# Scores of sparse attention made one step earlier, and three early weight splits put into other steps

## The chip, the cores and the metric

The kernel runs on one core of a Trainium2 chip. The metric is the device time of one launch in microseconds (us), as the median of several runs; lower is better. One further execution was profiled, and the rows shown below are its trace. The engines are named PE (matrix multiplications, with PEld for its weight loads), DVE (vector engine), ACT (scalar engine), POOL (GpSimd) and SP (which issues most DMAs).

## The reference

Block-sparse attention and, on its output, a mixture of experts. Cut to what matters:

```python
B, H, S, D = 4, 8, 768, 64                 # 24 blocks of 32 rows
scores = q @ k.T / sqrt(D)
mask: key blocks 0 and 23, the own block and its neighbours, three random blocks per query block;
      query blocks 0 and 23 see every key
attn = exp(scores - max); attn /= attn.sum + 1e-9; x = attn @ v
x -> (3072 tokens, 512); logits = x @ w_gate (8 experts); e = argmax(logits)
gate = softmax(logits)[e]; eom = sigmoid(x @ w_output_gate)[e]
out = gate * eom * (relu(x @ w1[e]) @ w2[e])         # 512 -> 1024 -> 512
```

## The kernel before

**Two stages.** Attention runs first, to about 300 us. Each expert's tokens are then gathered into slots of 128 rows, and 28 slots go through the two layers of their expert, to the end. Weights and tokens are held there as a high and a low half in fp16. `w_h` (ACT, L924) makes the high half of a piece of weights, `w_l` (DVE, L930) the low one. Nine pieces are split during attention already, in two halves of 512 columns each, in steps that the table `AHEAD` (L53) lists: for each piece the steps of `w_h`, `w_l`, `w_h`, `w_l`.

**Steps.** Attention is done in two halves (`bp` 0 and 1), each for two of the four batches. A half has 8 dense units (the two query blocks that see everything) and 11 tiles (`i`) of two query blocks. A tile has four sparse units, two pairs; the units of a pair, the even and the odd one, differ in the batch (`b`), the pairs in the group of heads (`hg`). So there are 104 units, and unit m has its step m. A unit's operations are spread over steps by lags:

- step m: `pS`, the scores S on PE (L490); the first unit of a pair makes those of both, 32 matmuls. `dM`, the maximum (DVE, L497). `aE`, the exp (ACT, L502), which leaves P
- step m+2: `pT`, four transposes of P (PE, L441) into T; the copy of T to pt, on ACT for the even unit (`aH`, L448), on DVE for the odd one (`dL`, L450)
- step m+3: `pO`, the product with the values (PE, L515 for the common and window blocks, vc; L522 for the random ones, vt)
- step m+4: `aO`, the copy of O (ACT, L531), and `dD`, the sums of a row (DVE, L427); m+5: `fin`, their reciprocal (DVE, L540); m+6: `fin2`, the scaling into x (POOL)

Within a step the loop at L1181 to L1203 emits these in one fixed order: `pT`, `pS`, `aH`, the early hooks, `dM`, `dL`, `pO`, `aO`, `aE`, `dD`, `fin`, the other hooks, `fin2`. Every engine works its instructions off in the order in which they were emitted (`in_order`, L77); only semaphores let engines run apart.

**Hooks.** `at(step, f)` puts further work into a step: DMAs, gathers of keys and values, the splits of `AHEAD`, and the router. The keys of a tile lie in one of three rings `kr`: three random blocks each, copied by DVE (L381), ACT (L383) and POOL (L385), and the window's four, copied by DVE (`window_k`, L392 and L393). `lead` (L1062) says how many steps ahead. The random values vt are gathered by POOL's indirect DMA (`gather_v`, L403) into one of two buffers.

**The router's turn** of a finished tile of x: transposes xp (PE, L677), the cast to the high half (ACT, L679), the subtraction for the low half (DVE, L680), the logits lp (PE, L689 and L690), their sum lsum (DVE, L694). After every fourth tile follow the choice of experts on POOL and DVE and the sum of ranks rp (PE, L732 to L737).

**Banks.** Scores S share four PSUM banks with lp, rp and the transition's small tiles. T shares two banks with xp; the pool assigns them, not in strict turn. In a tile with a router's turn, xp stands in the last step of the tile before; the T of the first unit's step takes the bank that DVE's copy of the T before it (an odd unit's) frees, and the T of the next step takes that same bank once ACT has copied it. O has two banks of its own.

Of the kernel before, what the change touches and what calls it, by code (L numbers as in the profile page):

```python
# [49 lines left out]
PACE = -1, 0, 0, 2, 4, 7, 8, 9, 10, 11, 12, 13, 14, 15, 16, 17, 18  # L50

PLAN = 6, (20,)
AHEAD = ((73, 74, 77, 78), (81, 82, 85, 86), (89, 90, 93, 94), (96, 97, 97, 98), (97, 98, 98, 99), (99, 100, 100, 101),  # L53
         (100, 101, 101, 102), (101, 102, 102, 103), (103, 104, 104, 105))
FIN = ("_1_9_1_1", "_1_10_0_1", "_1_10_1_1")
T0 = 5
# [34 lines left out]
def tile_kernel(ctx, tc, q, k, v, sampled, wg, wcat, out):  # L91
# [911 lines left out]
    def at(n, f, *a):  # L1003
        hooks.setdefault(n, []).append((f, a))
# [45 lines left out]
    for bp in range(2):  # L1050
# [6 lines left out]
        for i in range(NPAIR):  # L1057
            u0 = o + 8 + 4 * i
            if bp or i != 1:
                at(u0 - 8, load_q, bp, i)  # L1060

            lead = 3 if bp or i > 1 else 0  # L1062
            for kind, n, ns in KC[bp]:
                at(u0 - n - lead if bp or i != 1 else u0 - min(n, 5), gather_k, bp, i, kind, ns)
            at(u0 - 3 - lead, window_k, bp, i)
            at(u0 - 5 + LAGS[2] if bp or i else 6, window_v, bp, i)
            at(u0 - 5 + LAGS[2] if bp or i > 1 else (8, 12)[i], gather_v, bp, i)
# [43 lines left out]
    for m, un in enumerate(units):  # L1111
        lags = LAGD if isinstance(un, Dense) else LAGS
        le, lt, lo = lags
        d = "0" if isinstance(un, Dense) else ""
        for lag, f in ((lt, "pT"), (0, "pS"), (lt, "aH"), (0, "dM"), (lt, "dL" + d), (lo, "pO"), (lo + 1, "aO"), (lo + 1, "dD"),
                       (le, "aE" + ("0" if le else "")), (lo + 2, "fin"), (lo + 3, "fin2")):
            sched.setdefault((min(m + lag, n + 2), f), []).append(getattr(un, f.strip("0")))

# [51 lines left out]

    for i, hl in enumerate(AHEAD):
        for m in range(2):
# [91 lines left out]
```

## Time and profile before

| | |
|---|---|
| median of 3 runs | 623.2 us (621.53 to 624.46) |
| profiled execution | 622.91 us, its span 621.0 us |
| mean granted PE clock | 0.970 |
| PE busy | 564.4 us (91%) |
| PEld busy | 391.3 us (63%) |
| DVE busy | 473.8 us (76%) |
| ACT busy | 435.5 us (70%) |
| POOL busy | 260.6 us (42%) |

A row of a timeline reads: start in us from the start of the span, duration, engine, line of the kernel, operation, what it writes and reads (sizes as partitions x elements, and how many instructions the row joins), and in square brackets how long the engine had stood idle and what ended that, by the profile. A releaser in brackets is the last semaphore that the profile saw, so it can name an instruction that had ended long before. A row of windows reads: the stretch, its length, then busy time and count of instructions of PE, PEld, DVE, ACT and POOL, the granted PE clock, a DMA share and GB/s. A row of waits reads: waiting operation, releaser, total time, how many, the longest.

### The profile page before, as it was taken

The page shows a single profiled execution, that of the slowest core. Times are in us where ns is not written, and L with a number is a line of the kernel's source. Part 1 is how long each engine was busy: PE and PEld are TensorE (multiplying, and loading weights), DVE is VectorE, ACT ScalarE, POOL GpSimd, SP SyncE. Part 2 cuts the span into 40 slices and gives each one's busy share as a digit, 9 for nine tenths or more (in the row PEclk, how much of TensorE's full clock was granted, in tenths as well). Part 3 has the DMA queues.
Part 4 walks back from the last instruction along what each step waited for, and adds up shares of the span by engine and source line. Part 5 has one row for each costly group of instructions (what it writes and reads, how often), then busy time and mean ns, then how long its engine had stood idle before and what let it go on. Part 6 is the DMA issues. An engine that isn't in the chain of part 4 may idle for free. (4 is left out here: it accounts for less than half of the span.)

```text
span 621.0 us, 22116 instructions
## 1 busy us (share of the span) xinstructions
PE 564.4 (91%) x8275; PEld 391.3 (63%) x8275; DVE 473.8 (76%) x934; ACT 435.5 (70%) x834; POOL 260.6 (42%) x324
## 2 busy tenths in 40 slices
PE   6799988989889888888979998999999999999996
PEld 4466655555556555555757776777777777777763
DVE  4587657567657567577689988899898989989891
ACT  1466657656557777677459887887888888788871
POOL 4575758765645766665332131131312122131311
PEclk8899989999889899998699999999999999999999
DMA  8986979795865866559227399359943935823491
GB/s 312 381 260 228 320 250 296 274 283 134 285 141 204 257 210 189 176 159 272 53 64 286 83 292 357 83 145 275 301 119 95 309 76 163 265 63 81 94 295 45
DMA packets 72859, 126.94 MB, mean 204 GB/s; under 512 B 38187, under 2 KB 44459, under 8 KB 72492
## 3 DMA queue, kind: packets, MB, share of 16 engines
q1 hardware_dynamic: 61004, 87.84, 47.9%
q0 software_dynamic: 11744, 37.64, 18.2%
q8 instruction: 67, 1.10, 0.7%
q14 instruction: 44, 0.36, 0.2%
HBM read 183.09 MB, written 20.49 MB: 328 GB/s over the span
## 5 line engine op out<-in xcount | busy, mean ns | idle before, releaser
L930 DVE SCALAR_TENSOR_TENSOR kr<-r,kr 128x1024 f16<-128x1024 f32 (+1 forms) x173 | 184.5, 1110 | 17.2 <-ACT kr L924 16.2
L924 ACT ACTIVATE kr<-r 128x1024 f16<-128x1024 f32 (+1 forms) x173 | 156.4, 960 | 0.8 <-DMA r<-in_wcat_dram 0.8
L941 PEld LDWEIGHTS <-kr 128*128 128x128 f16 x2004 | 125.9, 98 | 46.8 <-issue 9.2
L981 POOL DMA_INDIRECT out_dram<-yo,tab x28 | 29.7, 1059 | 213.2 <-ACT yo L978 191.1
L972 PE MATMUL y<-kr,hh 128*128 128x512 f16 x423 | 114.0, 379 | 0.4 <-DVE hh L959 0.4
L502 ACT ACTIVATE P<-S,mx 128x256 f32<-128x256 f32 x176 | 74.5, 478 | 46.1 <-DVE mx L497 42.4
L941 PE MATMUL h<-xb,kr 128*128 128x128 f16 x1344 | 93.3, 219 | 2.1 <-DMA xb<-qz 2.1
L497 DVE TENSOR_REDUCE mx<-S 128x2 f32<-128x512 f32 x88 | 59.9, 680 | 30.2 <-PE S L490 30.1
L930 DVE SCALAR_TENSOR_TENSOR ws<-r,ws 128x1024 f16<-128x1024 f32 (+1 forms) x60 | 67.8, 1167 | 8.7 <-ACT ws L924 7.1
L403 POOL DMA_INDIRECT vt<-vscr,vidx x44 | 46.8, 1063 | 55.7 <-PE O L522 45.0
L441 PE MATMUL T<-ident,P 128*128 128x128 f32 x352 | 58.7, 291 | 11.1 <-DVE den L540 6.6
L972 PEld LDWEIGHTS <-hh 128*128 128x128 f16 x594 | 50.0, 98 | 25.7 <-DVE hh L959 1.1
L490 PE MATMUL S<-kr,qz 64*32 64x256 f32 x1408 | 59.4, 400 | 4.3 <-issue 3.8
L924 ACT ACTIVATE ws<-r 128x1024 f16<-128x1024 f32 (+1 forms) x60 | 58.1, 1015 | 0.8 <-PE y L972 0.8
L941 PEld LDWEIGHTS <-ws 128*128 128x128 f16 x684 | 44.3, 100 | 16.9 <-issue 6.1
L952 ACT ACTIVATE hh<-h 128x512 f16<-128x512 f32 (+1 forms) x56 | 30.5, 545 | 33.6 <-PE h L941 31.0
L441 PEld LDWEIGHTS T<-ident,P 128*128 128x128 f32 x352 | 38.8, 145 | 18.0 <-issue 14.0
L522 PE MATMUL O<-vt,pt 128*32 128x65 f32 x1408 | 42.0, 229 | 8.6 <-issue 4.6
L515 PEld LDWEIGHTS O<-vc,pt 128*64 128x64 f32 x704 | 28.7, 140 | 31.2 <-issue 20.8
L680 DVE TENSOR_TENSOR xT<-xp,xT 128x512 f16<-128x512 f32 x24 | 16.6, 692 | 39.4 <-ACT xT L679 36.2
L972 PE MATMUL y<-ws,hh 128*128 128x512 f16 x171 | 46.0, 379 | 0.0
L515 PE MATMUL O<-vc,pt 128*64 128x65 f32 x704 | 41.1, 238 | 3.2 <-DVE den L427 1.3
(227 smaller groups left out, 931.1 us busy)
## 6 DMA issues: line engine op xcount, KB each, us to landing
r<-in_wcat_dram SPq DMA_DIRECT2D x240, 512.0 KB
vscr<-vn SPq DMA_DIRECT2D x12, 520.0 KB
qz<-in_q_dram SPq DMA_DIRECT2D x24, 256.0 KB
xscr<-xq SPq DMA_DIRECT2D x48, 128.0 KB
vc<-vscr SPq DMA_DIRECT2D x22, 260.0 KB
kn<-in_k_dram SPq DMA_DIRECT2D x2, 1536.0 KB
vs<-in_v_dram SPq DMA_DIRECT2D x6, 512.0 KB
kn<-in_k_dram SPq DMA_DIRECT2D x6, 512.0 KB
```

The lines of the kernel that those rows point to most:

```text
L403: nc.gpsimd.indirect_dma_start(t[:, s].rearrange("p b j w -> p (b j w)"), None, vscr[bp], bass.IndirectOffsetOnAxis(ap=vidx[:, i, s:s + 1] ...
L441: nc.tensor.transpose(pt[:, 128 * c:128 * c + 128], p[:, 128 * c:128 * c + 128], ident)
L490: nc.tensor.matmul(u.s[64 * h2 + 32 * qi:64 * h2 + 32 * qi + 32, hp], t[p, 64 * j + 32 * qi:64 * j + 32 * qi + 32], g[p, 1 - qi:3:1 + qi, ...
L497: nc.vector.tensor_reduce(mx, self.s, axis=AX.X, op=ALU.max, negate=True)
L502: nc.scalar.activation(p[:, 256 * hp:256 * hp + 256], self.s[:, hp], AF.Exp, bias=self.mx[:, hp:hp + 1])
L515: nc.tensor.matmul(o[64 * h2:64 * h2 + 64, hp, 0:VW], w[:, col:col + 64], cv[:, b, 4 * h2 + 2 * hg + hp], start=hp == 0, stop=False)
L522: nc.tensor.matmul(o[64 * h2 + 32 * qi:64 * h2 + 32 * qi + 32, hp, 0:VW], w[:, col:col + 32], av[:, qi, b, 4 * h2 + 2 * hg + hp], start=Fa ...
L924: nc.scalar.activation(w[:, 0, r], piece(n // 8, n % 8)[:, r], AF.Copy, scale=SW)
L930: nc.vector.scalar_tensor_tensor(w[:, 1, r], piece(n // 8, n % 8)[:, r], SW, w[:, 0, r], op0=ALU.mult, op1=ALU.subtract)
L941: nc.tensor.matmul(hps[n // 4][:, 128 * j:128 * j + 128], w[:, hl, 128 * c:128 * c + 128], x[:, c // 2, xl, c % 2], start=cnt == 0, stop=c ...
L952: nc.scalar.activation(hs[g][0], hps[g][:, 0:m], AF.Relu)
L972: nc.tensor.matmul(ys[s], a[:, m], w[:, l, 512:1024], start=n % 8 == 0 and cnt == 0, stop=n % 8 == 7 and cnt == 2)
```

## The change

Three edits. `pS` of the sparse units stands at lag -1 instead of 0: the scores of a pair are made in the step in front of the pair's first unit. `lead` becomes 4 instead of 3 (for tile 1 of the first half 1 instead of 0; tile 0 of the first half keeps 0), so the keys' copies move a step earlier with them. And in the first three entries of `AHEAD` each `w_l` stands two steps later; the `w_h` and the six other entries stay.

```diff
-AHEAD = ((73, 74, 77, 78), (81, 82, 85, 86), (89, 90, 93, 94), (96, 97, 97, 98), (97, 98, 98, 99), (99, 100, 100, 101),
+AHEAD = ((73, 76, 77, 80), (81, 84, 85, 88), (89, 92, 93, 96), (96, 97, 97, 98), (97, 98, 98, 99), (99, 100, 100, 101),
          (100, 101, 101, 102), (101, 102, 102, 103), (103, 104, 104, 105))
...
-            lead = 3 if bp or i > 1 else 0
+            lead = 4 if bp or i > 1 else 1 if i else 0
             for kind, n, ns in KC[bp]:
                 at(u0 - n - lead if bp or i != 1 else u0 - min(n, 5), gather_k, bp, i, kind, ns)
             at(u0 - 3 - lead, window_k, bp, i)
...
         le, lt, lo = lags
+
+        ls = 0 if isinstance(un, Dense) else -1
         d = "0" if isinstance(un, Dense) else ""
-        for lag, f in ((lt, "pT"), (0, "pS"), (lt, "aH"), (0, "dM"), (lt, "dL" + d), (lo, "pO"), (lo + 1, "aO"), (lo + 1, "dD"),
+        for lag, f in ((lt, "pT"), (ls, "pS"), (lt, "aH"), (0, "dM"), (lt, "dL" + d), (lo, "pO"), (lo + 1, "aO"), (lo + 1, "dD"),
```

What this does to the order of the engines shows in three places. The first is PE at tile 4 of the second half, four steps from the step of its first unit on. In the names, `S_1_4_0_1` is half 1, tile 4, batch 0, heads 1; the matmuls of one S alternate between the pair's two units, and of them the first row stands here. Before:

```order
L677 MATMUL xp14_5072<-ident_82,x1_1_4896 128x2x64 x4
L441 MATMUL T0_1_3_0_1_5079<-ident_82,P_1_3_0_1_4995 128x128 x4
L490 MATMUL S_1_4_0_0_5084<-kr1_180,qz2_186 32x256
...
L515 MATMUL O_1_3_1_0_5108<-vc1_183,pt0_1_3_1_0_5038 64x65 x4
...
L441 MATMUL T0_1_3_1_1_5154<-ident_82,P_1_3_1_1_5054 128x128 x4
...
L689 MATMUL lp14_5195<-wg32_91,xT14_5071 128x32
...
L441 MATMUL T0_1_4_0_0_5207<-ident_82,P_1_4_0_0_5123 128x128 x4
L490 MATMUL S_1_4_0_1_5212<-kr1_180,qz2_186 32x256
...
L441 MATMUL T0_1_4_1_0_5283<-ident_82,P_1_4_1_0_5178 128x128 x4
L515 MATMUL O_1_4_0_0_5292<-vc0_182,pt0_1_4_0_0_5230 64x65 x4
```

And with the change:

```order
L677 MATMUL xp14_5111<-ident_82,x1_1_4907 128x2x64 x4
L441 MATMUL T0_1_3_0_1_5118<-ident_82,P_1_3_0_1_5019 128x128 x4
L515 MATMUL O_1_3_1_0_5129<-vc1_183,pt0_1_3_1_0_5066 64x65 x4
...
L441 MATMUL T0_1_3_1_1_5165<-ident_82,P_1_3_1_1_5082 128x128 x4
L490 MATMUL S_1_4_0_1_5170<-kr1_180,qz2_186 32x256
...
L689 MATMUL lp14_5237<-wg32_91,xT14_5110 128x32
...
L441 MATMUL T0_1_4_0_0_5249<-ident_82,P_1_4_0_0_5144 128x128 x4
L515 MATMUL O_1_3_1_1_5258<-vc1_183,pt0_1_3_1_1_5190 64x65 x4
...
L441 MATMUL T0_1_4_1_0_5293<-ident_82,P_1_4_1_0_5207 128x128 x4
L490 MATMUL S_1_5_0_0_5298<-kr2_181,qz0_184 32x256
```

The scores of the tile's second pair (`S_1_4_0_1`) now stand ahead of the logits lp, one step earlier, and those of the next tile's first pair stand in this tile's last step. So between the T of steps 0 and 1 only an O is left, and the same between those of steps 2 and 3; an S stands between those of steps 1 and 2, and one between that of step 3 and the next tile's xp.

The second place is DVE in the same tile, from the maximum of its first unit to the copy of the last step. Before:

```order
L497 TENSOR_REDUCE mx_1_4_0_0_5106<-S_1_4_0_0_5084 128x2
...
L497 TENSOR_REDUCE mx_1_4_1_0_5159<-S_1_4_1_0_5085 128x2
L450 COPY pt0_1_3_1_1_5161<-T0_1_3_1_1_5154 128x512
...
L694 TENSOR_REDUCE lsum_187<-lp14_5195 128x16
L497 TENSOR_REDUCE mx_1_4_0_1_5232<-S_1_4_0_1_5212 128x2
...
L392 TENSOR_SCALAR kr0_179<-kn1_1061 128x256
L393 TENSOR_SCALAR kr0_179<-kn1_1061 128x768
L930 SCALAR_TENSOR_TENSOR ws0_4949<-r0_3611,ws0_4949 128x512
L497 TENSOR_REDUCE mx_1_4_1_1_5288<-S_1_4_1_1_5213 128x2
L450 COPY pt0_1_4_1_0_5290<-T0_1_4_1_0_5283 128x512
```

And with the change:

```order
L497 TENSOR_REDUCE mx_1_4_0_0_5127<-S_1_4_0_0_5046 128x2
...
L930 SCALAR_TENSOR_TENSOR ws0_4991<-r0_3635,ws0_4991 128x512
L497 TENSOR_REDUCE mx_1_4_1_0_5188<-S_1_4_1_0_5047 128x2
L450 COPY pt0_1_3_1_1_5190<-T0_1_3_1_1_5165 128x512
...
L392 TENSOR_SCALAR kr0_179<-kn1_1083 128x256
L393 TENSOR_SCALAR kr0_179<-kn1_1083 128x768
L694 TENSOR_REDUCE lsum_187<-lp14_5237 128x16
L497 TENSOR_REDUCE mx_1_4_0_1_5256<-S_1_4_0_1_5170 128x2
...
L497 TENSOR_REDUCE mx_1_4_1_1_5316<-S_1_4_1_1_5171 128x2
L450 COPY pt0_1_4_1_0_5318<-T0_1_4_1_0_5293 128x512
```

The window's copies (L392, L393) have gone from step 2 to step 1, and the weight split (L930) from step 2 to step 0. Nothing is added between the last two maxima.

The third place is PE behind a router sum, rp3 in tile 6 of the second half, with the semaphores that a row waits for in brackets. Before:

```order
L737 MATMUL rp3_5672<-cum4_192,ones_93 128x2
L441 MATMUL T0_1_5_1_1_5692<-ident_82,P_1_5_1_1_5575 128x128 [waits Activation_49]
L441 MATMUL T0_1_5_1_1_5692<-ident_82,P_1_5_1_1_5575 128x128 x3
L515 MATMUL O_1_5_0_1_5701<-vc1_183,pt0_1_5_0_1_5622 64x65 [waits DVE_49]
```

And with the change:

```order
L737 MATMUL rp3_5682<-cum4_192,ones_93 128x2
L441 MATMUL T0_1_5_1_1_5703<-ident_82,P_1_5_1_1_5603 128x128 [waits Activation_49]
L441 MATMUL T0_1_5_1_1_5703<-ident_82,P_1_5_1_1_5603 128x128 x3
L490 MATMUL S_1_6_0_1_5708<-kr0_179,qz1_185 32x256
L490 MATMUL S_1_6_1_1_5709<-kr0_179,qz1_185 32x256 [waits DVE_49,Activation_49]
```

The scores of the second pair now follow rp and T directly. Their second matmul waits for DVE and ACT, because rp has taken one bank of the four and it gets the bank of the tile's first unit, which that unit's exp has to have read.

## The prediction

> **What bounds the kernel now.** I read the windows by stage first, then the waits of each engine between 20 and 322 us, then the timelines of single tiles. A tile here is four sparse units in four steps, called step 0 to 3, counted from the step that takes the maximum of its first unit.
>
> ```profile
> 200.00:250.00 50.00, 42.43 (x919) 28.57 (x911) 33.35 (x101) 35.40 (x97) 34.31 (x43) 0.97 0.72 223
> 450.00:500.00 50.00, 50.00 (x553) 35.82 (x550) 45.89 (x47) 41.08 (x56) 9.90 (x8) 1.00 0.60 171
> ```
>
> From 322 us on PE has no idle time (second row, 50.00 of 50), and the change touches nothing there: what attention saves or loses moves that part as a whole. In attention (first row; the columns are PE, PEld, DVE, ACT, POOL) PE leads with 42.43 of 50 and idles 7.6. So the sum is made of PE's stops before 322 us.
>
> ```profile
> DVE mx L497 <- PE S L490: 30.1, 30, 2.5
> PE T L441 <- DVE den L540: 6.6, 10, 1.7
> PE T L441 <- issue: 2.3, 2, 1.4
> PE T L441 <- DVE mx L497: 1.3, 1, 1.3
> PE T L441 <- DVE den L427: 0.9, 1, 0.9
> ```
>
> The largest wait of DVE, 30.1 us for the scores S, is no loss by itself, since DVE isn't the bound. It counts where PE waits for DVE later: the transposes T stop PE for 6.6 + 2.3 + 1.3 + 0.9 = 11.1 us. One such tile, DVE and ACT first, then PE:
>
> ```profile
> 221.22 0.69 DVE L497 TENSOR_REDUCE mx<-S 128x2 f32<-128x512 f32 x1 [1.21 <-PE S L490]
> 221.95 0.84 ACT L502 ACTIVATE P<-S,mx 128x256 f32<-128x256 f32 x2 [0.32 <-DVE mx L497]
> 222.09 0.56 DVE L393 TENSOR_SCALAR kr<-kn 128x768 f32<-128x768 f32 x1
> 222.56 0.69 DVE L930 SCALAR_TENSOR_TENSOR ws<-r,ws 128x512 f16<-128x512 f32 x1
> 223.16 0.69 DVE L497 TENSOR_REDUCE mx<-S 128x2 f32<-128x512 f32 x1
> 223.76 0.69 DVE L450 COPY pt<-T 128x512 f32<-128x512 f32 x1
> 223.15 0.66 PE L677 MATMUL xp<-ident,x 128*128 128x128 f32 x4
> 224.59 0.63 PE L441 MATMUL T<-ident,P 128*128 128x128 f32 x4 [0.79 <-DVE den L540]
> ```
>
> In step 2 DVE stands 1.21 us without scores, then does the maximum, the window of keys (L392, L393), a weight split (L930), the next maximum and the copy of step 3's T, without a gap. The copy ends at 224.45; the T of the next step 0, which takes the copied bank, starts 0.14 later, 0.79 late. Three of these stops lie past 270 us, where weight splits that stay where they are fill DVE:
>
> ```profile
> 278.22 0.63 PE L441 MATMUL T<-ident,P 128*128 128x128 f32 x4 [1.71 <-DVE den L540]
> 291.19 0.63 PE L441 MATMUL T<-ident,P 128*128 128x128 f32 x4 [0.98 <-DVE den L540]
> 293.50 1.12 PE L441 MATMUL T<-ident,P 128*128 128x128 f32 x4 [0.94 <-issue]
> ```
>
> **The change part by part.** The sum is made against the profiled execution's own 622.9 us (span 621.0), which lies 0.3 under the median 623.2.
>
> **Scores one step earlier, window out of step 2, three splits to step 0: the T stops go.** DVE then comes to step 2 with its scores made and without window and split. What is left ahead of the copy is two maxima and small work, so the copy ends as soon as its own T allows, and between T and the next T stand S, O and xp of step 3. PE's pace, start to start:
>
> ```profile
> 192.33 0.45 PE L515 MATMUL O<-vc,pt 128*64 128x65 f32 x8
> 193.08 0.66 PE L677 MATMUL xp<-ident,x 128*128 128x128 f32 x4
> 194.17 0.63 PE L441 MATMUL T<-ident,P 128*128 128x128 f32 x4 [0.43 <-DVE den L540]
> 198.55 0.64 PE L441 MATMUL T<-ident,P 128*128 128x128 f32 x4
> 199.12 1.09 PE L490 MATMUL S<-kr,qz 64*32 64x256 f32 x32
> 200.14 0.45 PE L515 MATMUL O<-vc,pt 128*64 128x65 f32 x8
> ```
>
> T takes 0.57, S 1.02, O 0.75. T, S and O of step 3 are thus 2.34 us, against 1.3 for T and its copy one behind the other (0.63 + 0.69 = 1.32 by the rows at 224.59 and 223.76): no stop remains. Of 11.1 us the three late ones (1.71 + 0.98 + 0.94 = 3.63) stay, 7.5 go. Ends: 0, if something else makes DVE late, and 7.5.
>
> **Values gathered a little earlier for their use.** POOL issues the gathers of vt when the O of step 2 two tiles ahead of their use is done; the O of step 3 needs them five steps later.
>
> ```profile
> 94.92 0.95 POOL L403 DMA_INDIRECT vt<-vscr,vidx  x1 [0.30 <-issue]
> 95.77 0.63 PE L441 MATMUL T<-ident,P 128*128 128x128 f32 x4 [0.85 <-DVE den L427]
> 104.88 0.43 PE L522 MATMUL O<-vt,pt 128*32 128x65 f32 x14 [1.27 <-issue]
> 84.32 0.43 PE L522 MATMUL O<-vt,pt 128*32 128x65 f32 x14 [2.69 <-DMA vt<-vscr,vidx]
> 135.45 0.43 PE L522 MATMUL O<-vt,pt 128*32 128x65 f32 x14 [1.22 <-DMA vt<-vscr,vidx]
> 203.78 0.43 PE L522 MATMUL O<-vt,pt 128*32 128x65 f32 x14 [1.62 <-issue]
> ```
>
> About 10 us pass from issue (94.92) to the matmul that had waited (104.88): the landing ends these four stops, 6.8 us together. In the changed order one more S (1.02 us) lies on PE between issue and use, and the T stops that lay there are gone. At 84.32 that is worth 1.02; at 104.88 1.02 - 0.85 = 0.17; at 203.78 1.02 - 0.43 = 0.59; at 135.45, between these, I take 0.6. Sum 2.4. Ends: 0, if the landing itself comes later, and 6.8.
>
> **New wait: T of step 1 behind T of step 0.** No S stands between them any more, and the later one takes the bank that ACT's copy of the earlier one frees. That copy is queued behind the router's cast (L679), which waits for xp.
>
> ```profile
> 105.24 0.66 PE L677 MATMUL xp<-ident,x 128*128 128x128 f32 x4
> 105.73 0.60 PE L441 MATMUL T<-ident,P 128*128 128x128 f32 x4
> 105.93 0.59 ACT L679 CAST xT<-xp 128x512 f16<-128x512 f32 x1 [1.02 <-PE xp L677]
> 106.43 0.59 ACT L448 COPY pt<-T 128x512 f32<-128x512 f32 x1
> 106.55 0.69 DVE L680 TENSOR_TENSOR xT<-xp,xT 128x512 f16<-128x512 f32 x1 [1.07 <-issue]
> ```
>
> Here ACT stood ready: cast 0.69 after xp's start, copy end at 107.02, 1.78 after it, plus the 0.14 above: 1.92. PE comes after xp (0.49 to 0.58), T and O 1.81 to 1.90 after it. That is a stop of 0 to 0.1, taken as 0.1 in 20 tiles: +2.0. ACT would have to be late for more (a rival below); at 224 us it was, its cast 2.2 us after xp, but because its exp had waited for the late maximum, which the change takes away. Queued behind the waiting T on PE are S and O of step 1, and DVE's and ACT's next units wait for them.
>
> **New wait: S for a bank, in the four tiles that hold a router sum.** The router sum rp takes one of four score banks in step 0, and the second matmul of the S in step 1 then gets the bank of the tile's first unit, whose exp was done long before and now comes first.
>
> ```profile
> 187.63 0.18 PE L732 MATMUL rp<-oh,tri 128*128 128x8 f16 x1
> 187.99 0.64 PE L441 MATMUL T<-ident,P 128*128 128x128 f32 x4
> ```
>
> From xp's start: cast at 0.69, router subtraction 0.62 later (105.93 to 106.55), maximum 0.60 later (as 223.16 to 223.76), exp 0.73 later (221.22 to 221.95) and 0.84 long, PE 0.14 later: 3.62. PE gets there after xp 0.58, T 0.57, O 0.75, rp 0.36 and T 0.57: 2.83. Stop 0.8, four times: +3.2; ends 0 (DVE has its maximum earlier) and, with ACT late by as much again, 4 x 1.6.
>
> **The rest.** ACT's and POOL's gathers of keys and DVE's window keep their count and their distance to the scores; both move a step. SP's order is unchanged, and so is each DMA. At the first step of each half the scores now stand ahead of a dense O and wait for a dense exp: between 0 and one S (1.02) each, +0.5 for both. Past 270 us the third split enters step 0 of a full DVE (+0.7 at most, its 0.69), while waits for scores go there too: 0.
>
> Sum: 622.9 - 7.5 - 2.4 + 2.0 + 3.2 + 0.5 = **618.7 us**.
>
> **A rule on the clock.** Two stretches behind such stops:
>
> ```profile
> 80.00:90.00 10.00, 7.32 (x124) 4.78 (x120) 5.58 (x15) 4.96 (x13) 6.38 (x8) 0.83 0.86 270
> 280.00:290.00 10.00, 9.21 (x172) 6.14 (x170) 8.92 (x24) 8.19 (x22) 4.79 (x5) 0.83 1.15 359
> ```
>
> The granted clock (third column from the end) is 0.83 in both; one holds the stop of 2.69 us that ended at 84.32, the other follows that of 1.71 that ended at 278.22. The Trainium skill (TensorE: Matmul & The Clock Gate, Part 1: The HAM clock gate) has the clock fall to half after an idle window of about 3.4 us; no stop quoted here is that long, so by it shortening them changes no clock and the sum stays. The trace agrees less: half speed has followed shorter stops.
>
> **The rivals.** A, the forecast: stops at T go, small new ones come, 618.7; own range 615 to 620.5.
>
> B, the waits change places: for it speaks that both new waits hang on the one chain xp, cast, subtraction, maximum, exp, and that the gathers' landing is a fixed 10 us. With 0.3 instead of 0.1 in 20 tiles (+4.0) and nothing won at the gathers (+2.4) it is 625.1 at most; with one of the two, 621 to 623. Against it: ACT's cast no longer waits for a late exp. Taken as 622.5.
>
> C, slower: ACT stays late in step 3. Its queue there holds a unit's exp (0.84) and a gather ahead of the cast. If the cast came as late as at 224 us (2.2 after xp instead of 0.69, so 1.5 late), T of step 1 would stop PE 1.5 us in each of 20 tiles, 30 us; with half of that, 15 - 2.0 more than in the sum: 631.7. It decides from 0.3 us a tile (6 us) for no gain and 0.5 for a loss. Against it: with scores a step ahead that exp's maximum is done before PE reaches xp.
>
> D, more than forecast: the four gather stops vanish whole (4.4 more) and two stretches at 0.83 run at full clock (10 x 0.17 = 1.7 each, 3.4): 610.9. That needs PE's new waits to be real, since they too give the gathers time.
>
> That the change doesn't do what it says I leave out: S stands a step earlier on PE in every tile.
>
> **How the numbers follow.** A 0.55, B 0.26, C 0.10, D 0.09. About 0.5% (3.1 us) is what a measurement tells from no change: faster is under 620.1, slower over 626.3. A lies under 620.1 in nine cases of ten (0.50) and D all (0.09); with a little of B that is 0.60. B's rest and A's give 0.30, C 0.10. The range 611 to 626 leaves out C and about half of D. The median's 0.3 above the profiled time is less than the shown runs differ among themselves (621.53 to 624.46), so 618.7 stands as the median too.
>
> **What would show it.** Right: T's waits for DVE before 270 us under 2 us in all, DVE's wait for S (30.1) under 10, the four gather stops shorter. T with a new wait of 0.1 in step 1 and S waiting 0.8 in four tiles. Wrong: T's waits stay near 11 us with ACT's copy as what ends them (C), or gather stops of the old size with T's gone (B); or PE's idle time before 322 us falls and the span doesn't, which would put the bound in what follows attention.

## The result, and the profile after

The changed kernel takes 647.3 us (median of 4 runs, 645.57 to 659.26) against 623.8 us (621.53 to 624.8) for the kernel before: ratio 1.0375, interval 1.0332 to 1.0418. (A median is over all executions; a ratio, here and below, leaves out those in a slower state, here the one of 659.26 us, and so can differ a little from the quotient of the medians.) It is slower, 21 us above the upper end of the range. The profiled execution took 648.88 us, its span 646.6, so 25.6 more than the span before. Part 1 of the page, after:

```profile
PE 573.5 (89%) x8275; PEld 398.9 (62%) x8275; DVE 478.6 (74%) x934; ACT 435.2 (67%) x834; POOL 259.2 (40%) x324
```

PE is busy 9.1 us longer (573.5 against 564.4), so it idles 16.5 us longer. The groups of instructions say where; first before, then after (the columns behind the bar are busy time, mean ns of one, and the idle time in front of them with what ended it):

```profile
L441 PE MATMUL T<-ident,P 128*128 128x128 f32 x352 | 58.7, 291 | 11.1 <-DVE den L540 6.6
...
L490 PE MATMUL S<-kr,qz 64*32 64x256 f32 x1408 | 59.4, 400 | 4.3 <-issue 3.8
...
L522 PE MATMUL O<-vt,pt 128*32 128x65 f32 x1408 | 42.0, 229 | 8.6 <-issue 4.6
```

```profile
L522 PE MATMUL O<-vt,pt 128*32 128x65 f32 x1408 | 54.1, 234 | 29.2 <-issue 29.0
...
L441 PE MATMUL T<-ident,P 128*128 128x128 f32 x352 | 61.4, 301 | 1.4 <-DVE den L427 1.3
...
L490 PE MATMUL S<-kr,qz 64*32 64x256 f32 x1408 | 53.3, 398 | 1.4 <-issue 1.0
```

The stops at T, on which the forecast rested, are gone: 11.1 to 1.4 us. But O's matmuls with the gathered values (L522) idle 29.2 us instead of 8.6 and are busy 54.1 instead of 42.0, together 32.7 us more, while S takes 9.0 less (59.4 + 4.3 against 53.3 + 1.4). The waits of PE between 20 and 330 us, after:

```profile
PE O L522 <- issue: 29.0, 51, 1.2
PE O L515 <- DVE den L427: 4.0, 7, 1.1
...
PE Od L610 <- issue: 3.0, 6, 1.2
...
PE T L441 <- DVE den L427: 1.3, 1, 1.3
...
PE S L490 <- ACT P L502: 0.4, 2, 0.2
```

51 stops of 0.6 us on average with "issue" as releaser: the profile shows no semaphore that PE waits for. It is not the old stop at a landing: in the tile shown next, all 256 packets of the values that O reads had landed by 220.8 us, counted from the packets of the trace, and O is stopped from 226.4 on. This tile, PE and POOL in the timeline after:

```profile
224.20 0.66 PE L441 MATMUL T<-ident,P 128*128 128x128 f32 x4
224.57 0.99 POOL L403 DMA_INDIRECT vt<-vscr,vidx  x1 [3.01 <-PE O L522]
224.79 1.09 PE L490 MATMUL S<-kr,qz 64*32 64x256 f32 x32
225.81 0.45 PE L515 MATMUL O<-vc,pt 128*64 128x65 f32 x8
225.87 0.94 POOL L403 DMA_INDIRECT vt<-vscr,vidx  x1 [0.30 <-issue]
226.19 0.24 PE L522 MATMUL O<-vt,pt 128*32 128x65 f32 x1
226.90 0.22 PE L522 MATMUL O<-vt,pt 128*32 128x65 f32 x1 [0.47 <-issue]
227.11 0.99 POOL L780 DMA_INDIRECT table<-vals,place  x1 [0.31 <-issue]
227.64 0.23 PE L522 MATMUL O<-vt,pt 128*32 128x65 f32 x1 [0.52 <-issue]
229.06 0.46 PE L522 MATMUL O<-vt,pt 128*32 128x65 f32 x13 [1.19 <-issue]
229.44 0.66 PE L677 MATMUL xp<-ident,x 128*128 128x128 f32 x4
```

From the first gather's start (224.57) PE still starts 32 + 8 + 1 = 41 matmuls, up to 226.19. Then it is let through one matmul at a time, 0.7 us apart (226.19, 226.90, 227.64), and runs on at 229.06, 4.5 us after the gather's start. The text below calls this the **hold**. The windows of the same stretch show what the other engines did:

```profile
226.00:227.00 1.00, 0.54 (x10) 0.26 (x8) 0.00 (x0) 0.56 (x2) 0.80 (x1) 1.00 1.06 256
227.00:228.00 1.00, 0.35 (x2) 0.11 (x1) 0.00 (x0) 0.00 (x0) 0.89 (x1) 1.00 0.63 99
228.00:229.00 1.00, 0.00 (x0) 0.11 (x1) 0.00 (x0) 0.00 (x0) 0.97 (x3) 1.00 0.95 361
```

From 228 to 229 PE, DVE and ACT do nothing but one weight load, at a granted clock of 1.00 (third column from the end); only POOL works and data moves. The same kind of tile before, with two PE rows that the prediction shows (xp at 223.15, T at 224.59) left out:

```profile
222.18 1.32 POOL L403 DMA_INDIRECT vt<-vscr,vidx  x1 [1.54 <-PE O L522]
222.40 0.45 PE L515 MATMUL O<-vc,pt 128*64 128x65 f32 x8
222.78 0.44 PE L522 MATMUL O<-vt,pt 128*32 128x65 f32 x16
...
223.81 0.94 POOL L403 DMA_INDIRECT vt<-vscr,vidx  x1 [0.31 <-issue]
...
225.15 1.09 PE L490 MATMUL S<-kr,qz 64*32 64x256 f32 x32
225.56 1.03 POOL L780 DMA_INDIRECT table<-vals,place  x1 [0.17 <-issue]
226.18 0.45 PE L515 MATMUL O<-vc,pt 128*64 128x65 f32 x8
226.56 0.77 PE L522 MATMUL O<-vt,pt 128*32 128x65 f32 x16
```

Here PE starts 8 + 16 + 4 + 4 = 32 matmuls behind the gather before S at 225.15, 2.97 us after the gather's start: dense matmuls of T and xp, and a stop that waits for DVE. It comes to its forty-second matmul only when about 3.3 us have passed. The hold is in the kernel before too, and shows where PE comes to that number before its end: in the tile whose first gather starts at 113.04, T has no stop, and S is stopped after 44 matmuls until 116.08, 3.04 us after the gather's start:

```profile
115.02 0.69 PE L490 MATMUL S<-kr,qz 64*32 64x256 f32 x11
116.08 2.21 PE L490 MATMUL S<-kr,qz 64*32 64x256 f32 x21 [0.36 <-issue]
```

### The profile page after: what moved, and what is told of

The parts are those of the page before. It is cut to its first block, busy times and chain, and to the rows that moved or that the text cites. A ratio compares the mean times of both kernels' runs of the same rounds, so it can differ in the third digit from the quotient of the medians.

```text
span 646.6 us, 22115 instructions
## 1 busy us (share of the span) xinstructions
PE 573.5 (89%) x8275; PEld 398.9 (62%) x8275; DVE 478.6 (74%) x934; ACT 435.2 (67%) x834; POOL 259.2 (40%) x324
## 5 line engine op out<-in xcount | busy, mean ns | idle before, releaser
L930 DVE SCALAR_TENSOR_TENSOR kr<-r,kr 128x1024 f16<-128x1024 f32 (+1 forms) x173 | 184.4, 1109 | 17.3 <-ACT kr L924 16.4
L502 ACT ACTIVATE P<-S,mx 128x256 f32<-128x256 f32 x176 | 74.5, 480 | 28.1 <-DVE mx L497 25.3
L522 PE MATMUL O<-vt,pt 128*32 128x65 f32 x1408 | 54.1, 234 | 29.2 <-issue 29.0
L930 DVE SCALAR_TENSOR_TENSOR ws<-r,ws 128x1024 f16<-128x1024 f32 (+1 forms) x60 | 71.8, 1233 | 8.3 <-ACT ws L924 7.8
L403 POOL DMA_INDIRECT vt<-vscr,vidx x44 | 43.3, 985 | 50.3 <-PE O L522 40.9
L441 PE MATMUL T<-ident,P 128*128 128x128 f32 x352 | 61.4, 301 | 1.4 <-DVE den L427 1.3
L522 PEld LDWEIGHTS O<-vt,pt 128*32 128x32 f32 x1408 | 31.5, 113 | 43.3 <-issue 36.9
L490 PE MATMUL S<-kr,qz 64*32 64x256 f32 x1408 | 53.3, 398 | 1.4 <-issue 1.0
L515 PEld LDWEIGHTS O<-vc,pt 128*64 128x64 f32 x704 | 29.2, 143 | 32.8 <-issue 15.0
L679 ACT CAST xT<-xp 128x512 f16<-128x512 f32 x24 | 14.0, 585 | 49.1 <-PE xp L677 49.1
```

Source lines behind the costliest of these rows:

```text
L403: nc.gpsimd.indirect_dma_start(t[:, s].rearrange("p b j w -> p (b j w)"), None, vscr[bp], bass.IndirectOffsetOnAxis(ap=vidx[:, i, s:s + 1] ...
L441: nc.tensor.transpose(pt[:, 128 * c:128 * c + 128], p[:, 128 * c:128 * c + 128], ident)
L490: nc.tensor.matmul(u.s[64 * h2 + 32 * qi:64 * h2 + 32 * qi + 32, hp], t[p, 64 * j + 32 * qi:64 * j + 32 * qi + 32], g[p, 1 - qi:3:1 + qi, ...
L502: nc.scalar.activation(p[:, 256 * hp:256 * hp + 256], self.s[:, hp], AF.Exp, bias=self.mx[:, hp:hp + 1])
L522: nc.tensor.matmul(o[64 * h2 + 32 * qi:64 * h2 + 32 * qi + 32, hp, 0:VW], w[:, col:col + 32], av[:, qi, b, 4 * h2 + 2 * hg + hp], start=Fa ...
L930: nc.vector.scalar_tensor_tensor(w[:, 1, r], piece(n // 8, n % 8)[:, r], SW, w[:, 0, r], op0=ALU.mult, op1=ALU.subtract)
```

## The experiments

The theory behind the first experiments: POOL's indirect gathers hold PE for a time, and the change puts PE's work into it. The rivals: the values land late; PE's order at that point is bad in itself; one of the three edits does it by another way; POOL's order does it. Diffs are against the changed kernel where nothing else is said. Ratios are to the kernel before on the same chip.

**What stands in the hold, and whether the landing ends it.** e1 puts the scores behind the O of their step:

```diff
-        for lag, f in ((lt, "pT"), (ls, "pS"), (lt, "aH"), ...
+        for lag, f in ((lt, "pT"), (ls, "pS0" if ls else "pS"), (lt, "aH"), ...
-        run("aE0", "dL0", "dM", "dL", "pO", "aO", "aE", "dD", "fin")
+        run("aE0", "dL0", "dM", "dL", "pO", "pS0", "aO", "aE", "dD", "fin")
```

> The changed kernel with one difference: the scores S of the sparse units stand behind the O of the same step instead of ahead of it. Theory G (the indirect gather of values that POOL issues behind the O of step 2 slows PE from about 1.6 to 4.6 us after its issue, and S moved the O of step 3 into that time): the O of step 3 starts again under 1 us after the issue, idle time ahead of L522 falls from 29 to 9 us or less as before the change, the T stops stay under 3 us, time 612 to 622. Theory L (the values of this tile land too late): the O stands a microsecond earlier, so its waits stay or grow, 645 or more. Theory P (PE is slowed in that time whatever it does): the stops move to S, 640 to 650.

649.08 us, ratio 1.0468 (1.0382 to 1.0553). The stops have left L522 and stand at S. Groups of e1:

```profile
L490 PE MATMUL S<-kr,qz 64*32 64x256 f32 x1408 | 78.8, 399 | 16.8 <-issue 15.7
```

S is busy 78.8 instead of 53.3 and idles 16.8 instead of 1.4. S reads no gathered values, so no landing holds it: PE is stopped at whatever it has reached. That is what theory P expected, not G.

e2 leaves the gathers out from the third tile of each half on, e3 replaces them by plain DMAs of SP, as many bytes, but not the rows chosen:

```diff
     def gather_v(bp, i):
+        if i >= RV:
+            vt[bp, i] = vt[bp, i - RV]
+            return
```

```diff
-            nc.gpsimd.indirect_dma_start(
-                t[:, s].rearrange("p b j w -> p (b j w)"), None, vscr[bp],
-                bass.IndirectOffsetOnAxis(ap=vidx[:, i, s:s + 1], axis=0))
+            nc.sync.dma_start(t[:, s].rearrange("p b j w -> p (b j w)"), vscr[bp][128 * s:128 * s + 128, :])
```

> The changed kernel without the gathers of values from the third tile of each half on: those tiles use the values of the first two, so their part of the output is wrong. G: no stops of L522 in tiles without a gather, its idle time under 6 us (29 before), time about 647 - 23 - 10 = 614. D (SP's transfers of the same moment, xscr, weights and qz, slow PE): L522's idle time stays over 20 us and the time over 640.

> The changed kernel with each indirect gather of POOL replaced by a plain DMA of SP that brings as many rows of the same length to the same place (the wrong rows, so the output is wrong). If the data in flight slows PE: L522's idle time stays over 15 us, in the time in which the rows land. If the indirect gather's issue on POOL and its descriptors do: under 6 us, time under 625, but for waits of SP's queue behind O.

615.2 and 611.33 us (one run each) where the kernel before takes 619.28. The wait list of e3 has 4.3 us for O with vt instead of 29.0:

```profile
PE O L520 <- issue: 4.3, 6, 1.9
```

So the loss hangs on POOL's indirect gathers, not on the bytes and not on PE's order alone. In e2 O with vt idles 0.2 us in all.

**Which edit brings it.** e4 has the old `AHEAD`; e5 has the window's copies back in their old step; e6 has both, so only the scores and the copies of the random keys are early. e7 and e12 are the kernel before with one edit alone: the window a step earlier, or the new `AHEAD`.

```diff
 e4, e6
-AHEAD = ((73, 76, 77, 80), (81, 84, 85, 88), (89, 92, 93, 96), ...
+AHEAD = ((73, 74, 77, 78), (81, 82, 85, 86), (89, 90, 93, 94), ...
 e5, e6
-            at(u0 - 3 - lead, window_k, bp, i)
+            at(u0 - 3 - (3 if bp or i > 1 else 0), window_k, bp, i)
 e7, against the kernel before
-            at(u0 - 3 - lead, window_k, bp, i)
+            at(u0 - 3 - (4 if bp or i > 1 else 1 if i else 0), window_k, bp, i)
```

> The changed kernel with the weight splits where they were. G: the O stops stay (over 20 us), time within 1% of the changed kernel's 647. Theory W (the splits in step 0 delay something that PE waits for): L522's stops fall by half or more, time under 635.

> The changed kernel with the window's copies of keys (L392, L393) a step later, in step 2, where they stood before the change; scores, the other keys and the splits as changed. Theory K (DVE's window copies, which ran beside the issue of the gather in step 2, spread it out: 1.32 us instead of 0.99, and so kept PE supplied): first gathers last 1.3 us again in most tiles, L522's idle time falls from 29 to under 12 us, time 610 to 625. Theory I (PE gets only some 85 instructions from the gather's issue until 3 to 4.5 us later, and only PE's own pauses in the T stops hid that): L522's idle time stays over 20 us, time 635 to 650.

> As the kernel with the window back in step 2, and the weight splits where they were too: the scores (and the other keys' copies) a step earlier are all that is left of the change. Theory K: split and window both beside the gather, L522's idle time under 10 us, T stops 5 us at most, time 610 to 622. Theory I: L522 idle over 20 us, time 630 to 645.

> The kernel before with one difference: the window's copies of keys a step earlier, in step 1; scores and splits as before. Theory K: first gathers last 0.99 us, PE is held in the microseconds behind them as in the changed kernel, time up by 10 us or more (630 to 645). Theory I: PE still has its T stops or is paced by scores as before, time within 1% of before.

> The kernel before with the three early weight splits moved two steps, as in the change, and nothing else. If the splits by themselves cost what the changed kernel lost more than the one with the splits back (some 0.7%): 624 to 630 beside a before of 620. If they only cost where scores are early: within 0.3% of before.

| kernel | us | ratio | idle before L522 |
|---|---|---|---|
| e4 | 638.41 | 1.0313 (1.0266 to 1.036) | 25.1 |
| e5 (profile of its longest run, 652.56) | 644.77 | 1.0379 (1.0294 to 1.0464) | 28.1 |
| e6 | 637.93 | 1.0284 (1.0169 to 1.0398) | 26.6 |
| e7 | 621.9 | 1.0017 (0.9975 to 1.006) | 5.0 |
| e12 | 625.68 | 1.0083 (1.0047 to 1.012) | 6.2 |

The early scores and keys bring the hold by themselves (e6); window and splits don't. The splits in step 0 cost 0.8% in e12 alone; the differences 0.6% (e4 against the changed kernel) and 0.9% (e6 against e5) agree, but their intervals overlap. e7 also shows what a shorter stop at T is worth; its groups:

```profile
L490 PE MATMUL S<-kr,qz 64*32 64x256 f32 x1408 | 68.9, 395 | 5.7 <-issue 3.5
...
L441 PE MATMUL T<-ident,P 128*128 128x128 f32 x352 | 57.1, 286 | 5.4 <-DVE den L540 2.5
```

T idles 5.4 instead of 11.1, but S is busy 68.9 instead of 59.4: PE reaches S sooner, is let through it slowly (in the tile whose first gather starts at 203.94, S is stopped after 43, 44 and 46 matmuls, until 4.57 us after the gather's start), and the time is unchanged. In the kernel before, the stops at T lay inside the hold: of its twelve over 0.3 us, ten end 1.9 to 3.6 us after a tile's first gather.

**What ends the hold.** e8 issues only one gather per tile (half of its values are then old). e11 puts a useless matmul of 128x128x512, 22.4 us in all, ahead of the O that is stopped. e13 lets POOL touch the O's weights, so that L522 cannot start before about 2.5 us after the first gather.

```diff
 e8
-        for s in range(2):
+        for s in range(1 if i >= RV else 2):
 e11
+            if hg == 0 and b == 0 and i >= 1:
+                nc.tensor.matmul(ob, ident, w, start=True, stop=True)
 e13
+    def touch(m):
+        p = units[m].pt[0][:, 0:1]
+        nc.gpsimd.tensor_copy(p, p)
+            if i > 1:
+                at(u0 - 2, touch, u0 - 4)
```

> The changed kernel with only the first of the two gathers of a tile, from the third tile of each half on (half of the values are old, the output is wrong). If each gather holds PE by itself: L522's idle time about half of 29, 12 to 17 us, and PE free again about 3 us after the issue in every tile, time 628 to 634. If the first alone does it: 25 or more. If only the second: under 6.

> The changed kernel with one useless matmul more (128x128 by 128x512, fp32, some 1.2 us by the 0.62 us of each half of L968's) ahead of the O of step 3 in the 20 tiles from the second of each half on, its result overwritten: one instruction that keeps PE's instructions waiting for a microsecond in the time after the gathers' issue, as the T stops did before. Theory I (what counts is the number of PE instructions between the gather's issue and 3 to 4.5 us later): L522's idle time falls from 29 to under 18 us and the time by 0 to 15 us, to 632 to 647, though 24 us of work are added. If the stops are waits of a fixed end that instructions have no part in: idle falls by the added 24 us at most and the time stays within 4 us of 647. If O simply waits as before: 665 to 672.

> The changed kernel with a wait for PE in place of the stops: POOL copies one column of pt onto itself right behind the second gather of a tile (from the third tile of each half on), and the L522 of step 3's O, which reads that column, has to wait for it, until about 2.4 us after the first gather's issue, as T did before the change in the tiles that were not held. Theory Q (a PE that stands at a semaphore until the gathers are issued is not held afterwards): the wait costs some 0.8 us in 18 tiles, stops without a visible cause fall from 29 to under 10 us, time 622 to 634. Theory R (the hold has its fixed end, 3 to 4.5 us after the issue, whether PE waits or not): stops behind the wait remain, waits and stops together 28 us or more, time 642 to 652.

e8: 630.26 us (one run, before 621.23), idle before O's vt matmuls 12.3 us. These numbers are what was expected, but not for the reason given, that each gather holds PE by itself: the six tiles with the one gather and no scatter (L780, an indirect DMA too) near it have no stop at all, and the stops stand where the scatter starts 1.3 to 1.8 us behind the gather (nine tiles), until 2.8 to 3.2 us after the gather's start. So the end goes with the number of indirect DMAs in a row, by about 1.5 us each: none seen behind one, 3.0 us behind two, 4.5 behind two gathers and a scatter, 6.0 behind the four of e8's last tile, 7.4 behind the five of the changed kernel's last tile (first gather at 294.40). e11: 643.33, ratio 1.0378 (1.0322 to 1.0435), no slower than the changed kernel for 22.4 us more work on PE:

```profile
PE O L524 <- issue: 15.2, 26, 1.2
```

e13: 649.41, ratio 1.0489 (1.0404 to 1.0574); stops come after the pause all the same. The pause itself is 16 stops of 0.8 us, 12.9 in all, of which the list puts only four down to POOL; of the 29.6 us that L522 idles in all, some 16.5 are the hold behind it:

```profile
PE O L522 <- issue: 26.2, 47, 1.2
PE O L522 <- POOL pt L1005: 3.2, 4, 0.8
```

So the end of the hold is a time counted from POOL's indirect DMAs; PE may work or wait until then for about the same price. The pause does not use the hold up.

**Gathers without indirect DMA.** e9 and e10 are the changed kernel and the kernel before with the gathers as eight plain DMAs of SP per tile, their rows from registers (the change in the index set-up is left out here):

```diff
-            nc.gpsimd.indirect_dma_start(...)
+            for g, r in enumerate(rows):          # three register rows and an edge row
+                nc.sync.dma_start(
+                    t[32 * g:32 * g + 32, s].rearrange("p b j w -> p (b j w)"), vscr[bp][r, :])
```

> The changed kernel with the indirect gathers of POOL replaced by eight DMAs of SP per tile, one for each block of 32 rows, whose row numbers SP loads into registers; all values are right. Theory I (each indirect gather holds PE to some 85 instructions until 3 to 4.5 us after its issue): L522's idle time falls from 29 to under 8 us, T stops stay under 3, time 606 to 618. If the bytes of the gather in flight were the cause: over 20 us idle, 635 or more. SP's own queue may add waits for values of up to 5 us.

> The kernel before with the same replacement. Theory I: the gathers cost little here, T stops of about 10 us stay, 612 to 622, so that the change is worth 3 to 10 us where no gather holds PE. If the change is slower by itself (rival C of the prediction): this kernel is faster than the changed one with the replacement by 5 us or more.

660.7 and 666.52 us, over 40 above what was expected, ratios 1.0789 (1.072 to 1.0858) and 1.0817 (1.0696 to 1.0937) to the kernel before, which took 612.59 there. In both, L522's line now waits for real landings; e9:

```profile
PE O L541 <- DMA vt<-vscr: 35.4, 20, 4.0
```

This is no way out, and it tells little of the hold, because the kernel before was as fast there as on the chip of e14 to e17 below. With these gathers the changed order is not the slower one.

**POOL's order, and the chip.** With `lead` 4 POOL's copies of keys (L385) stand a step earlier, so in eight more tiles (nine instead of one) the scatter L780 of the router directly follows the two gathers, as in the tile shown. e14 gives the kernel before POOL's new order, e15 the changed kernel POOL's old one; in e16 the scatter stands two steps later, behind arithmetic of POOL; e17 has the edits of e15 and e16, with the old `AHEAD`.

```diff
 e14, against the kernel before; e15 and e17 the same with + and lead == 4
-                at(u0 - n - lead if bp or i != 1 ...
+                at(u0 - n - lead - (lead == 3 and kind == "pool") if bp or i != 1 ...
 e16, e17, e18
-                        at(t0 + t5 + 1 + (4 if g < 4 ...
+                        at(t0 + t5 + 1 + 2 * (g < 4) + (4 if g < 4 ...
```

> The kernel before with POOL's copies of keys (L385) a step earlier, so that POOL works in exactly the order of the changed kernel; PE's order is that of before. Theory P, POOL's order decides the hold (behind the two gathers the scatter L780 now follows directly in eight more tiles): stops without a releaser before 322 us grow from 14 us to 25 or more in sum and the time goes to 630-642. Theory E, PE's order decides (scores and transposes between the gathers and O of step 3): PE's stops stay within 5 us of before and the time within 620-627.

> The changed kernel with POOL's copies of keys back in their old step, so that POOL works in exactly the order of the kernel before; PE's order is the changed one. Theory P: the hold goes back towards what it was, idle before L522 from 29 to 8-15 us, time 625-635. Theory E: idle before L522 stays over 22 us, time 640-650.

> The changed kernel with the scatters L780 of the first 16 tiles two steps later, so that arithmetic of POOL stands between gathers and scatter. Theory P (the count of indirect DMAs in a row sets the end of the hold): with two in a row it ends near 3.05 us instead of 4.5 in some nine tiles, idle before L522 16-20 us, time 632-639. Rival S (each indirect DMA holds PE by itself): stops of the same sum turn up behind the moved scatter, time 643-652.

> Scatters two steps later and POOL's copies of keys in their old step, on the changed kernel with the old places of the three splits (638.4 by itself). Theory P: hold near 3.05 us at most, idle before L522 10-16 us, time 620-630. Theory E with rival S: 635-642.

| kernel | us | ratio | idle before L522 |
|---|---|---|---|
| e14 | 614.64 | 1.0032 (0.9972 to 1.0092) | 7.6 |
| e15 | 612.73 | 0.997 (0.9904 to 1.0037) | 4.6 |
| e16 | 611.73 | 1.0008 (0.996 to 1.0056) | 6.3 |
| e17 | 612.71 | 1.0019 (0.9968 to 1.007) | 6.0 |

All four equal the kernel before, which took 614.36 us on this chip, and the expectations can't be read as meant: the hold is nearly absent whatever the order, also in the tiles between 64 and 102 us, in which e15 and e16 issue the same instructions on PE, POOL and DVE in the same order as the changed kernel. So the last run took the kernel of e16 to another chip.

> The kernel of e16 once more, which makes another chip likely. In e14 to e17, which shared one chip, the stops without a releaser were nearly gone whatever the order of POOL and PE, also in the tiles from 64 to 102 us, in which e16 and the changed kernel issue the same instructions in the same order. Theory chip: the hold belongs to some chips; where the kernel before takes 619-624 us, as on those of the first thirteen runs that showed the hold, this kernel takes 630-652 with 15 us or more idle before L522, and where the kernel before takes 612-615 it takes 609-615 again. Theory order: the moved scatter removes the hold on every chip; idle before L522 stays under 8 us and the ratio within 0.99-1.01 whatever the kernel before takes.

There the kernel before took 621.83 us, and the same kernel 627.56 (624.84 to 630.21), ratio 1.012 (1.0 to 1.024). PE's waits in e16 and, behind it, in e18:

```profile
PE O L522 <- DMA vt<-vscr,vidx: 4.6, 4, 2.2
PE O L515 <- DVE den L427: 4.0, 4, 1.4
PE T L441 <- DVE den L540: 4.0, 2, 2.7
...
PE O L522 <- issue: 1.7, 2, 1.4
```

```profile
PE O L522 <- issue: 14.7, 29, 1.1
```

1.7 us against 14.7 for the same instructions. A tile of e16, and the same place in e18:

```profile
225.99 0.98 POOL L403 DMA_INDIRECT vt<-vscr,vidx  x1 [2.76 <-PE O L522]
226.20 1.09 PE L490 MATMUL S<-kr,qz 64*32 64x256 f32 x32
227.23 0.45 PE L515 MATMUL O<-vc,pt 128*64 128x65 f32 x8
227.61 0.43 PE L522 MATMUL O<-vt,pt 128*32 128x65 f32 x16
```

```profile
222.86 0.99 POOL L403 DMA_INDIRECT vt<-vscr,vidx  x1 [1.97 <-PE O L522]
223.08 1.09 PE L490 MATMUL S<-kr,qz 64*32 64x256 f32 x32
224.10 0.45 PE L515 MATMUL O<-vc,pt 128*64 128x65 f32 x8
224.48 0.24 PE L522 MATMUL O<-vt,pt 128*32 128x65 f32 x1
225.13 0.22 PE L522 MATMUL O<-vt,pt 128*32 128x65 f32 x1 [0.40 <-issue]
225.86 0.49 PE L522 MATMUL O<-vt,pt 128*32 128x65 f32 x14 [0.51 <-issue]
```

Up to the forty-first matmul the two agree; then e18 is held until 225.86, 3.0 us after the gather's start, and e16 runs through. The scatter, now 4.2 us behind the gather in e18, brings no hold by itself, so the rival "each indirect DMA holds PE" falls, as it does by e8's tiles. Where it directly follows the gathers the hold lasts 4.5 us (changed kernel), where it doesn't 3.0; in the two tiles of e18 in which it still starts 3.0 and 3.1 us behind the first gather, the stops again last until 4.5. Idle before L522 is 15.1 instead of 29.2 and the ratio 1.012 instead of 1.0375, below the 630 to 652 us expected. These two ratios are from two chips, so their difference is only roughly the price of the scatters.

The count that fits this: matmuls that PE has started 2.3 us after a tile's first gather, median over the tiles from the second of each half on, counted from the single instructions of the trace.

| kernel | matmuls by 2.3 us | the hold |
|---|---|---|
| before | 29 | reached in few tiles, and late |
| changed | 44.5 | reached at about 1.7 us |
| e1 | 43 | reached |
| e18 | 43 | reached |
| e15, chip without hold | 58 | none to reach |

Where there is a hold, PE first stops at 42 to 46 matmuls (each with its weight load) in most tiles (33 to 49 in all, the fewest where dense units stand there). The kernel before comes to about that number only as the hold ends, at some 3.1 us; the changed one puts the 32 short matmuls of S right behind the gathers, and has used them up 1.4 us earlier.

The prices agree with that, as far as times from different chips can be compared. The kernel before takes 614.36 us on the chip without the hold and 619 to 624 on those with it, 5 to 9 more. The changed order takes 611.33 to 615.2 without its indirect gathers (e3, e2), 611.73 to 612.73 on the chip without the hold (e16, e15), and 647.3 with both, 32 to 36 more. The difference, some 23 to 31 us, holds the 23.5 measured. No version tried that computes with the right values beats the kernel before.

## Why the prediction was wrong, point by point

**What bounds the kernel** held as far as it went: the stops of PE before 322 us make the difference. But a stop "for" DVE at T also filled time in which PE could not have run on. A wait is put down to the one that came last, and behind T's semaphore the hold stood unseen. Its trace was there, though: the group of S in the profile of before has 3.8 us of idle time with only "issue" behind it, some of it stops like that at 116.08, and no part of the prediction takes it up.

**The T stops go** held as a mechanism: 7.5 of 11.1 us were forecast to go, 9.7 went, and DVE's wait for scores (30.1) is no longer in the list. That more went is partly the hold's doing, since PE came later to T: without it, T still idles 3.9 (e15) to 5.2 us (e16), about the 3.6 that the forecast had left. It was worth nothing where there is a hold (e7: T 5.7 less, time unchanged). So three of the prediction's signs of being right came true (T's waits under 2 us, DVE's wait for S gone, the waits for a landing gone) while the time got worse.

**Values gathered a little earlier for their use** is the step that failed. It counted the additional S between the gathers' issue and their use only as time for the landing, a gain of 2.4 us, and put at nothing what the gathers do to PE while POOL issues them. That S is what uses PE's matmuls up: in place of the -2.4, O with the gathered values takes 32.7 us more (29.2 - 8.6 idle, 54.1 - 42.0 busy); S, which had borne part of the hold before (59.4 us busy, against 53.0 in e14 without it), takes 9.0 less. Its ends, 0 and -6.8, had no room for a loss, though nothing excluded one. The four stops themselves were probably read rightly, also the two with only "issue" behind them: those end 10.0 and 10.3 us after the second gather of the tile before (94.92 and 193.52), the two with a named landing 11.3 and 10.4, and only 11 matmuls had started in them since the tile's own gather, far from 42. No wait for a landing is left in the list after; the tiles there last longer.

**T of step 1 behind T of step 0**, +2.0, and **S for a bank**, +3.2, were too dear: T has no wait for ACT's copy left in the list, and S waits 0.4 us for the exp in two places. The groups after show why rival C was far off as well:

```profile
L679 ACT CAST xT<-xp 128x512 f16<-128x512 f32 x24 | 14.0, 585 | 49.1 <-PE xp L677 49.1
```

ACT stands ready 49.1 us in all for xp, in 22 of the 24 casts. Part of that is PE's delay by the hold, but without the hold T's waits for ACT's copy are 0.3 us at most too (e15 to e17). C had the right sign and about a third of the size (8.8 of 24 us), by a mechanism that isn't there.

**The three splits** were left at nothing before 270 us. e12 alone measures +0.8% (about 5 us); O of the common blocks waits more for DVE there (L515, 3.5 us against 1.3 before; 4.0 in the changed kernel, 1.4 in e4 with the old splits). That the split now stands ahead of the sums of a row in step 0 would explain it; no run shows this by itself.

**The rest, B and D.** B's sign in the trace, stops at the gathers with T's gone, came several times larger than B had it, and not by its fixed landing. D's condition, real new waits, didn't come. On the rule of the clock: the mean granted clock fell from 0.970 to 0.959 (0.88 from 210 to 220 us), though none of the new stops lasts over 1.2 us; the Trainium skill's idle window of about 3.4 us (TensorE: Matmul & The Clock Gate, Part 1: The HAM clock gate) is not reached by any single one, and the trace again agrees less.

**What remains without the hold** is no forecast gain either. e15 to e17, whose orders on PE are those of the change, stand at 0.997 to 1.0019 of the kernel before; the forecast's 0.7% lies inside e15's interval and outside the two others. T idles less there (5.2 us in e16 against 9.2 in e14, which has PE's old order), O of the common blocks more (L515, 7.4 and in e15 12.3 against 4.6).

Three things stay open. The changed kernel itself was not run on a chip without the hold; e15 and e16 differ from it in POOL's order from about 102 us on. The scores were never made early without the keys' copies, so these two are not told apart. And whether the hold belongs to a chip or to a condition it is in at the time is not told; for the latter speaks that the record gives e9, e10 and e18 the same chip number, and the kernel before took 612.59 us with the first two and 621.83 with e18, about an hour later.

## What to carry to other kernels

A stop whose releaser the profile doesn't name is a cost of unknown cause: bound it on both sides, and look at what else ran when it began, here always POOL's indirect DMAs about 2 us earlier. Before work is pulled forward, look at what stands between it and the nearest indirect DMAs: few long matmuls there cost nothing here, many short ones did, and three indirect DMAs in a row cost more than two. Removing a wait gains only if the engine could have gone on, which a trial that shortens this wait alone tells (e7).

## What the runs showed of the hardware

In the runs with the hold PE stops, in most tiles of the changed order, 1.6 to 1.7 us after the start of the first of two indirect gathers, when it has started 42 to 46 matmuls with their weight loads. It is then let through a few at a time about 0.72 us apart, until 3.0 us (two indirect DMAs in a row) or 4.5 us (a scatter directly behind the two gathers) after the gather's start; behind one alone no stop was seen (e8). It looks as if PE's supply of instructions were cut off while POOL has indirect DMAs prepared, and PE ran on what it had in stock; this is argued, not shown. The Trainium skill (Runtime: NRT & Kernel Launch, Instruction fetch mechanics) gives PE room for 2048 instructions, refilled in blocks and mostly out of sight; a stock of some 86 instructions is far less. The page after lists such blocks as packets of the queues called instruction (q8: 67, 1.10 MB); none of these queues has a packet between 224.1 and 232.5 us, so the hold that ended at 229.06 did not end with the arrival of a block.

The same instructions took 627.56 us on one chip and 611.73 on another, while the kernel before took 621.83 and 614.36: a difference of 1 to 2% depended on which chip, or in which condition of it, the kernels ran.

The first gather lasts 1.32 us in the tile before, in which DVE's copy L393 (222.09, 0.56 long) runs beside it, and 0.99 in the tile after, where that copy has gone to another step. The Trainium skill (SBUF — State Buffer, SBUF: two separate sides) says that GpSimd can't write its descriptors while DVE holds the port that both share; these two rows agree. A copy that starts behind the gather did not lengthen it: in e5, where L393 starts 0.05 us after the gather at 226.38, this gather lasts 0.98. So e5 did not bring the long gathers back and doesn't test whether they matter; e7 does. Five of its 22 first gathers last over 1.2 us, against eleven in the kernel before, and its time is the same, so short gathers alone cost nothing.
